# Sine passes of a gate side by side, and a second PSUM bank for the attention units of the lead

## The chip, the core and the metric

One core of a Trainium2 chip runs the kernel. The metric is the time of one execution on the device in microseconds, the median of several. Names of engines: PE is TensorE (PEld its weight loads), ACT ScalarE, DVE VectorE, POOL GpSimd, SP the queue that starts the transfers.

## What is computed

Three layers follow each other: attention that keeps the 32 best scores of each row, a layer with the activation h cos(h), and eight experts that all see every token, weighted by a matrix P that is normalised eight times by rows and columns.

```python
def _attn_ref(q, k, v):                      # (4, 8, 576, 64)
    scores = scale * np.matmul(q, k.transpose(0, 1, 3, 2))
    kth = np.partition(scores, -32, axis=-1)[..., -32:-31]
    scores = np.where(scores >= kth, scores, -1000000000.0)
    scores = scores - np.max(scores, axis=-1, keepdims=True)
    attn = np.exp(scores)
    attn = attn / (np.sum(attn, axis=-1, keepdims=True) + 1e-09)
    return np.matmul(attn, v)
...
x = attn_out.transpose(0, 2, 1, 3).reshape(2304, 512)
h = x @ w_in                                 # (512, 2048)
x = (h * np.cos(h)) @ w_out                  # (2048, 512)
...
for e in range(8):                           # w1 (8, 512, 1024), w2 (8, 1024, 512)
    out += P[:, e:e + 1] * (np.maximum(x @ w1[e], 0.0) @ w2[e])
```

## The kernel before

The 2304 tokens are 18 tiles of 128. The first three are the **lead** (LEAD = 3): their attention and their first layer run ahead of everything, in plain fp32, so that the experts have input early. The first layer's weights arrive in a wide format and are decoded meanwhile by DVE, ACT and POOL (lines 348 to 353) into win_s and wout_s.

An attention **unit** is one head of one tile: 128 rows of scores. A lead tile has eight units, and `att_tile` emits each: two score matmuls into the bank ps_s (line 469), each copied out by ACT (475); eight passes on DVE that find the 32nd largest score (477 to 481); two ACT passes that mask and exponentiate (483, 484); a normalisation on POOL (488); four transposes on PE into the bank ps_t and an ACT copy of them to at_f (493, 497); a fifth transpose of the last 64 columns into ps_t and its copy (the same lines); then, in `attention_tile`, five matmuls with the values, again into ps_t (550), and an ACT copy into the tile's x_f (554). Through ps_t each of these steps waits for the one before, and the next unit for this one.

The first layer of a lead tile is `moe1_tile_a` and `moe1_tile_b`. Part a multiplies x_f with win_s in four blocks of 512 columns, each four matmuls (647) and a copy to hs (649). Two blocks make one half of 1024 columns, and on each half runs `gate`: POOL, POOL and DVE reduce the angle (610 to 612), ACT takes the absolute value and the sine (613, 614), and DVE multiplies (617). Eight transposes of a half (657) and their copies (660) fill gT. Part b runs 16 matmuls with wout_s into the one bank y3 (669), copies the result (671), transposes it (676) and splits it into x2fh and x2fl (683, 684). Sine and exponential have different tables on ACT, so a sine between two exponentials brings two table loads.

When the three lead tiles are through, the **fill** (the experts on the lead's tokens, matmuls of lines 393 to 395) starts and gives PE work beside the attention of the other tokens; its first matmul reads x2fh of all three tiles. The attention of the other tokens uses buffers that are only free after the lead's last value product. Later, about 640 to 740 us, a part of the first layer for 512 tokens runs between two fills, with the attention beside it.

What sets the order is `Plan`: every instruction is put down with its engine, an assumed cost, the buffers (or parts of them) that it reads and writes, and a priority by engine and class of work (the table PRIORITY; smaller goes first). `issue` then walks through an assumed time, takes on each engine the ready instruction of the smallest priority, and writes the program out in the order so found. Where it sees PE without work in the first 230 us, it puts in **heartbeats**: single 128x128 matmuls of constants whose result nobody reads (`pl.beat`, line 1085), so many that they fill about 0.65 of the gap. At run time each engine follows its own list in order; the real waits are semaphores, which the framework below derives from the buffers.

Of the kernel before, what the change touches and what calls it, by code (L numbers as in the profile page):

```python
# [14 lines left out]
AF = mybir.ActivationFunctionType  # L15
# [12 lines left out]
CLASSES = ("first attention", "first mlp", "decode", "attention", "mlp")  # L28
PRIORITY = {
    "PE": (0, 1, 9, 0.5, 3),  # L30
    "ACT": (0, 0, 0, 2, 1.5),
    "DVE": (1, 0, 0.5, 2, 0),
    "POOL": (0, 0.5, 1, 1.5, 2),
    "SP": (0, 1, 0.5, 2, 3),
# [213 lines left out]
def fused_kernel(tc, kq, vv, w_in, w_out, w_gate, w1, w2, out, B=4):  # L248
# [32 lines left out]
    def put(eng, cost, emit, reads=(), writes=(), func=None, nbytes=0):  # L281
        return add(eng, cost, emit, reads, writes, PRIORITY[eng][CLASSES.index(work)], func, nbytes)
# [171 lines left out]
    def att_tile(stats, dests, plain=None):  # L454
# [34 lines left out]
        pt = lambda: ps_t.ap.rearrange("p (c t) -> p c t", c=4)  # L489
        for c0, c1, p in ((0, 4, 128), (4, 5, 64)):  # L490
            def tr(c0=c0, c1=c1, p=p):
                for c in range(c0, c1):
                    T_.transpose(pt()[:p, c - c0, :], ex.ap[:, c * 128 : c * 128 + p], ident.ap)  # L493

            put("PE", 109.0 * (c1 - c0), tr, [ex, ident], [ps_t])
            if plain:
                put("ACT", act_ns((c1 - c0) * 128, psum=True), lambda c0=c0, c1=c1, p=p: A_.activation(at_f.ap[:p, c0:c1, :], pt()[:p, 0 : c1 - c0, :], AF.Copy),
                    [ps_t], [(at_f, c0, c1)])
            for r0, rn, hd, t0 in dests:
                ath, atl = hd["ath"], hd["atl"]  # L500
                tv = slice(t0, t0 + rn)
                hv = lambda ath=ath, c0=c0, c1=c1, p=p, tv=tv: ath.ap[:p, c0:c1, tv]
                if c0:

                    lb, lv = ath, lambda ath=ath, tv=tv: ath.ap[64:128, 4:5, tv]
                else:
                    lb, lv = atl, lambda atl=atl, tv=tv: atl.ap[:, :, tv]
                sv = lambda c0=c0, c1=c1, p=p, r0=r0, rn=rn: pt()[:p, 0 : c1 - c0, r0 : r0 + rn]
# [20 lines left out]
    def attention_tile(t):  # L529

        nonlocal work
        work = "first attention"
        x_f, q = xf_r(), qp_r()
        s0 = t * 128
        dma(lambda: q.ap, lambda: kq[0:H, 0:64, 1, s0 : s0 + 128].rearrange("h d s -> d h s"), 1 << 18, writes=[q], slow=True)
        for pr in range(H // 2):
            k, v = kq_r(), vp_r()
            hs = slice(2 * pr, 2 * pr + 2)
            dma(lambda k=k, hs=hs: k.ap[0:64], lambda hs=hs: kq[hs, 0:64, 0, :].rearrange("h d s -> d h s"), 512 * S, writes=[k], slow=True)
            dma(lambda v=v: v.ap, lambda hs=hs: vv[hs].rearrange("h p c d -> p h c d"), 128 * 2560, writes=[v])  # L540
            for j in range(2):
                at_f = at_r()
                for _ in range(AHEAD[t]):
                    next(parts, None)
                att_tile([], [], dict(q=q, k=k, at=at_f, h=2 * pr + j))

                def av(v=v, j=j, at_f=at_f):
                    for c in range(5):
                        p = 64 if c == 4 else 128
                        T_.matmul(ps_t.ap[:64, :128], v.ap[:p, j, c, :], at_f.ap[:p, c, :], start=c == 0, stop=c == 4)  # L550

                put("PE", 1100.0, av, [v, at_f], [ps_t])
                r = slice(64 * j, 64 * j + 64)
                put("ACT", act_ns(128, psum=True), lambda pr=pr, r=r: A_.activation(x_f.ap[r, pr, :], ps_t.ap[:64, :128], AF.Copy), [ps_t], [(x_f, pr, pr + 1)])
        work = "mlp"
        return x_f

# [46 lines left out]
    def gate(hs, rr, n=1024):  # L604

        (hb, hv), (rb, rv) = hs, rr
        tt = tt_r()
        tv = lambda: tt.ap[:, :n]
        e, f, c = ("POOL", G_, 85.0 + 0.7 * n) if eng_r == "POOL" else ("DVE", V, dve_ns(n, True))
        put(e, c, lambda: f.tensor_scalar(tv(), hv(), 1.0 / TWO_PI, MAGIC, op0=ALU.mult, op1=ALU.add), [hb], [tt])  # L610
        put(e, c, lambda: f.tensor_scalar(rv(), tv(), -MAGIC, -TWO_PI, op0=ALU.add, op1=ALU.mult), [tt], [rb])
        put("DVE", dve_ns(n), lambda: V.tensor_tensor(rv(), rv(), hv(), op=ALU.add), [hb, rb], [rb])
        put("ACT", act_ns(n), lambda: A_.activation(rv(), rv(), AF.Abs), [rb], [rb])
        put("ACT", act_ns(n, ap=True), lambda: A_.activation(rv(), rv(), AF.Sin, scale=-1.0, bias=cols.ap[:, 0:1]), [rb, cols], [rb], func="sin")
        (hb, _, _), (rb, _, _) = hb, rb
# [20 lines left out]
    def moe1_tile_a(t, x_f):  # L636
# [1 line left out]
        nonlocal work  # L638
        work = "first mlp"
        gT = gT_r()  # L640
        for b0 in (0, 2):
            hs, rr = hs_r(), rr_r()
            for i in range(2):
                b = b0 + i
                pb = hb()
                for c in range(4):
                    put("PE", 4 * mm_ns(512), lambda c=c, b=b, pb=pb: T_.matmul(pb.ap, x_f.ap[:, c, :], win_s.ap[:, c, b * 512 : b * 512 + 512], start=c == 0, stop=c == 3),
                        [(win_s, c * 4 + b, c * 4 + b + 1), (x_f, c, c + 1)], [pb])
                put("ACT", act_ns(512, psum=True), lambda i=i, hs=hs, pb=pb: A_.activation(hs.ap[:, i * 512 : i * 512 + 512], pb.ap, AF.Copy), [pb], [(hs, i * 512, i * 512 + 512)])
            gate(wide_of(hs), wide_of(rr))  # L650
            for i in range(2):
                tb = trb()
                f = 4 * (b0 + i)
# [46 lines left out]
    def moe1(p, lag):  # L700
# [15 lines left out]
        for f0 in range(0, NF1, 2):  # L716
            hs, rr = hs_r(), rr_r()
            for i in range(2):
# [8 lines left out]
                if len(pend) > lag:  # L727
                    second(*pend.pop(0))
            gate(wide_of(hs, 2 * n), wide_of(rr, 2 * n), 2 * n)
            for i in range(2):  # L730
                gh, gl = gh_r(), gl_r()
                split_cols((gh, lambda gh=gh: gh.ap[:, :n]), (gl, lambda gl=gl: gl.ap[:, :n]), ((rr, i * n, i * n + n), lambda i=i, rr=rr: rr.ap[:, i * n : i * n + n]), n, eng=eng_g)
# [349 lines left out]
                for _ in range(4):  # L1082
                    next(sums, None)
    mixed_second(acc, *pend.pop(0))
    pl.beat = (lambda: T_.matmul(ps_g.ap[:, 0:128], ones.ap, ident.ap, start=True, stop=True)), 220.0, 230e3
    with tc.manual_schedule():
        pl.issue()
    pl.close()
# [35 lines left out]
```

## Time and profile before

| | |
|---|---|
| median of 3 runs | 2369.33 us (2368.64 to 2369.57) |
| profiled execution | 2372.1 us, of which span 2370.0 us |
| PE busy | 2326.2 us (98%) |
| DVE, ACT, POOL busy | 1817.3, 1357.3, 1243.0 us |
| mean granted PE clock | 0.995 |
| first fill matmul | 254.56 us after the span's start |

The rows further down come from one execution. Times are microseconds from the span's start unless marked ns. An engine's busy time in a stretch says how full it is; a bracket behind an instruction says how long its engine sat idle before it, and what ended that.

### The profile page before, as it was taken

How to read it: one execution, taken by the hardware profiler on the slowest of the kernel's cores; microseconds unless marked ns; L12 is line 12 of the kernel's file. 1: busy time of each engine (PE TensorE's matmuls, PEld its weight loads, DVE VectorE, ACT ScalarE, POOL GpSimd, SP SyncE). 2: the span in 40 equal slices, each digit the busy share in tenths (PEclk: the TensorE clock that was granted, in tenths of full speed). 3: DMA queues.
4: the chain of work that ended last, by engine and by line, in shares of the span. 5: the costliest groups of instructions: out<-in, count | busy, mean ns of one | idle time of the engine just before them, and what ended most of it. 6: DMA issues, size and time to landing. Idle time of an engine off the chain costs nothing.

```text
span 2370.0 us, 34117 instructions
## 1 busy us (share of the span) xinstructions
PE 2326.2 (98%) x11383; PEld 1923.5 (81%) x11383; DVE 1817.3 (77%) x3340; ACT 1357.3 (57%) x2724; POOL 1243.0 (52%) x1320
## 2 busy tenths in 40 slices
PE   7999999999989999999999999999999999999999
PEld 5555898988867888888888897888888888888887
DVE  6995999999989999994177786876666666666665
ACT  6987888888877777775376675222223222222221
POOL 6754878887886666664501036433333344444440
PEclk8999999999999999999999999999999999999999
DMA  8741555554432343333443432122222221111101
GB/s 254 218 137 36 167 157 158 158 168 153 141 93 83 119 120 120 118 93 107 125 125 103 121 117 70 41 76 76 77 84 78 79 67 36 36 36 36 36 23 49
DMA packets 152464, 242.27 MB, mean 102 GB/s; under 512 B 14624, under 2 KB 61808, under 8 KB 152288
## 3 DMA queue, kind: packets, MB, share of 16 engines
q1 hardware_dynamic: 152288, 240.10, 33.8%
q8 instruction: 89, 1.46, 0.3%
q14 instruction: 87, 0.71, 0.1%
HBM read 208.18 MB, written 31.87 MB: 101 GB/s over the span
## 4 chain that ended last, share of the span: by engine, by line
PE 84%; DVE 6%; POOL 4%; ACT 3%; DMA 2%; issue 1%; SPq 0%; POOLq 0%; DVEq 0%; ACTq 0%
PE y L393 12%; PE y L395 12%; PE y L394 12%; PE g L393 4%; PE g L395 4%; PE g L394 4%; PE t L493 3%; PE h L393 3%; PE h L395 3%; PE h L394 3%; PE t L519 1%; PE s L465 1%; PE y L404 1%; PE y L405 1%; PE y L408 1%
## 5 line engine op out<-in xcount | busy, mean ns | idle before, releaser
L368 POOL TENSOR_TENSOR wlo<-raw,whi 128x512 fp32r<-128x512 f32 x336 | 446.8, 1335 | 150.3 <-ACT whi L366 114.6
L481 DVE MAX8 m<-wk 128x8 f32<-128x576 f32 x432 | 319.3, 750 | 3.6
L968 DVE SCALAR_TENSOR_TENSOR acc<-y,P,acc 128x512 f32<-128x512 f32 x308 | 229.2, 748 | 103.6 <-PE y L395 103.4
L366 ACT ACTIVATE whi<-raw 128x512 fp32r<-128x512 f32 x416 | 258.1, 626 | 77.6 <-PE y L395 31.7
L480 DVE MATCH_REPLACE8 wk<-m,wk 128x576 f32<-128x576 f32 x288 | 214.2, 744 | 2.1
L393 PE MATMUL y<-whi,gh 128*128 128x512 f32 x448 | 181.8, 406 | 0.0
L395 PE MATMUL y<-whi,gl 128*128 128x512 f32 x448 | 176.2, 393 | 0.0
L393 PE MATMUL y<-gh,xh 128*128 128x512 f32 x450 | 175.9, 391 | 0.1
L394 PE MATMUL y<-wlo,gh 128*128 128x512 f32 x448 | 175.6, 392 | 0.0
L394 PE MATMUL y<-gl,xh 128*128 128x512 f32 x450 | 175.1, 389 | 0.0
L395 PE MATMUL y<-gh,xl 128*128 128x512 f32 x450 | 175.1, 389 | 0.0
L493 PE MATMUL t<-ident,ex 128*128 128x128 f32 (+1 forms) x720 | 128.0, 276 | 12.7 <-POOL ex L488 3.1
L475 ACT ACTIVATE sc<-s 128x288 f32<-128x288 f32 x288 | 116.1, 403 | 36.6 <-PE s L466 25.1
L488 POOL TENSOR_SCALAR ex<-ex,m 128x576 f32<-128x576 f32 x144 | 108.2, 751 | 45.4 <-DVE m L487 40.5
L493 PEld LDWEIGHTS t<-ident,ex 128*128 128x128 f32 (+1 forms) x720 | 84.5, 135 | 55.5 <-issue 9.4
L511 ACT ACTIVATE ath<-t 64x128 fp32r<-64x128 f32 (+3 forms) x272 | 104.5, 396 | 38.2 <-PE t L493 36.1
L477 DVE MAX8 m<-sc 128x8 f32<-128x576 f32 x144 | 107.5, 746 | 20.4 <-ACT sc L475 20.3
L483 ACT ACTIVATE ex<-sc,m 128x576 f32<-128x576 f32 x144 | 110.9, 770 | 18.4 <-DVE m L481 18.2
L484 ACT ACTIVATE ex<-ex,m 128x576 f32<-128x576 f32 x144 | 111.3, 773 | 4.6 <-POOL m L482 0.5
L480 DVE MATCH_REPLACE8 wk<-m,sc 128x576 f32<-128x576 f32 x144 | 106.9, 742 | 0.2
L393 PEld LDWEIGHTS y<-gh,xh 128*128 128x128 f32 x450 | 84.5, 188 | 18.6 <-DVE acc L964 0.8
L395 PE MATMUL y<-gh,gl 128*128 128x512 f32 x254 | 99.5, 392 | 0.0
(378 smaller groups left out, 7037.4 us busy)
## 6 DMA issues: line engine op xcount, KB each, us to landing
raw<-in_w_dram SPq DMA_DIRECT2D x384, 256.0 KB, 2.7
kq<-in_kq_dram SPq DMA_DIRECT2D x40, 576.0 KB, 3.9
raw<-win_d SPq DMA_DIRECT2D x64, 256.0 KB, 3.1
raw<-wout_d SPq DMA_DIRECT2D x64, 256.0 KB, 2.7
y_d<-st SPq DMA_DIRECT2D x56, 256.0 KB, 2.9
raw<-y_d SPq DMA_DIRECT2D x56, 256.0 KB, 2.7
d_raw<-in_w_in_dram SPq DMA_DIRECT2D x16, 512.0 KB, 5.2
d_raw<-in_w_out_dram SPq DMA_DIRECT2D x16, 512.0 KB, 4.4
```

What stands on the lines that cost most here:

```text
L366: put("ACT", act_ns(n), lambda: A_.activation(hv(), rv(), AF.Copy), [rb], [hb])
L368: put(e, c, lambda: f.tensor_tensor(lv(), rv(), hv().bitcast(F32), op=ALU.subtract), [rb, hb], [lb])
L393: T_.matmul(o(), ah(), bh(), start=start, stop=False)
L394: T_.matmul(o(), ah(), bl(), start=False, stop=False)
L395: T_.matmul(o(), al(), bh(), start=False, stop=stop)
L475: put("ACT", act_ns(288, psum=True), lambda c=c: A_.activation(sc.ap[:, c], o(), AF.Copy), [ps_s], [(sc, c.start, c.stop)])
L480: put("DVE", 669, lambda r=r, src=src: V.match_replace(wk.ap, mc(8 * r, 8), src.ap, LOWEST), [src, (m, 8 * r, 8 * r + 8)], [wk])
L481: put("DVE", 669, lambda r=r: V.max(mc(8 * r + 8, 8), wk.ap), [wk], [(m, 8 * r + 8, 8 * r + 16)])
L483: put("ACT", act_ns(S, ap=True), lambda: A_.activation(ex.ap, sc.ap, AF.Prelu, scale=-1.0, bias=mc(31), alpha=TINY), [sc, (m, 24, 32)], [ex])
L484: put("ACT", act_ns(S, ap=True) + 93.0, lambda: A_.activation(ex.ap, ex.ap, AF.Exp, scale=-0.125 / TINY, bias=mc(32), accum_out=mc(33)), [ ...
L493: T_.transpose(pt()[:p, c - c0, :], ex.ap[:, c * 128 : c * 128 + p], ident.ap)
L968: put("DVE", 663, lambda y=y, av=av, pcol=pcol: V.scalar_tensor_tensor(av(), y.ap, pcol(), av(), op0=ALU.mult, op1=ALU.add), [y, P, a], [a])
```

## The change

The gate is cut in two functions. `gate` now ends with the absolute value, and `gate_end` has the sine and the multiplication. A lead tile runs its four blocks and both `gate`s first, and then both `gate_end`s; the first sine is made to read the buffers of both halves (`also`), so that it waits for both absolute values. The priority of ACT's work of the class "first mlp" (the lead's first layer) goes from 0 to -1, ahead of the lead's attention. In the lead's units the fifth transpose goes to columns 0 to 255 of the bank ps_g, and the value product to columns 256 to 511 of it; ps_t keeps the first four transposes. Heartbeats, which wrote ps_g, now write columns 384 to 511 of ps_s, the bank of the scores. The later first layer calls both functions one behind the other.

```diff
-    "ACT": (0, 0, 0, 2, 1.5),
+    "ACT": (0, -1, 0, 2, 1.5),
...
         for c0, c1, p in ((0, 4, 128), (4, 5, 64)):
-            def tr(c0=c0, c1=c1, p=p):
+            bank = ps_g if plain and c0 else ps_t
+            pt = lambda bank=bank: bank.ap.rearrange("p (c t) -> p c t", c=4)
+
+            def tr(c0=c0, c1=c1, p=p, pt=pt):
...
-            put("PE", 109.0 * (c1 - c0), tr, [ex, ident], [ps_t])
+            put("PE", 109.0 * (c1 - c0), tr, [ex, ident], [(bank, 0, 256) if plain and c0 else bank])
...
-                        T_.matmul(ps_t.ap[:64, :128], v.ap[:p, j, c, :], at_f.ap[:p, c, :], start=c == 0, stop=c == 4)
+                        T_.matmul(ps_g.ap[:64, 256:384], v.ap[:p, j, c, :], at_f.ap[:p, c, :], start=c == 0, stop=c == 4)
...
         put("ACT", act_ns(n), lambda: A_.activation(rv(), rv(), AF.Abs), [rb], [rb])
-        put("ACT", act_ns(n, ap=True), lambda: A_.activation(rv(), rv(), AF.Sin, scale=-1.0, bias=cols.ap[:, 0:1]), [rb, cols], [rb], func="sin")
+
+    def gate_end(hs, rr, n=1024, also=()):
+
+        (hb, hv), (rb, rv) = hs, rr
+        put("ACT", act_ns(n, ap=True), lambda: A_.activation(rv(), rv(), AF.Sin, scale=-1.0, bias=cols.ap[:, 0:1]), [rb, cols, *also], [rb], func="sin")
...
-        for b0 in (0, 2):
-            hs, rr = hs_r(), rr_r()
...
-            gate(wide_of(hs), wide_of(rr))
+        halves = [(hs_r(), rr_r()) for _ in range(2)]
+        for b in range(4):
+            hs, rr = halves[b // 2]
...
+            if i:
+                gate(wide_of(hs), wide_of(rr))
+        for b0, (hs, rr) in zip((0, 2), halves):
+            gate_end(wide_of(hs), wide_of(rr), also=[wide_of(r)[0] for _, r in halves[1:]] if not b0 else ())
...
             gate(wide_of(hs, 2 * n), wide_of(rr, 2 * n), 2 * n)
+            gate_end(wide_of(hs, 2 * n), wide_of(rr, 2 * n), 2 * n)
...
-    pl.beat = (lambda: T_.matmul(ps_g.ap[:, 0:128], ones.ap, ident.ap, start=True, stop=True)), 220.0, 230e3
+    pl.beat = (lambda: T_.matmul(ps_s.ap[:, 384:512], ones.ap, ident.ap, start=True, stop=True)), 220.0, 230e3
```

The program's order changes with it on every engine. Three places follow. Line numbers move by some lines: 469, 475, 483 and 484 stay, 493 becomes 495, 497 becomes 499, 550 becomes 552, 554 becomes 556, 613 becomes 615, 614 becomes 620, 647 becomes 653, 649 becomes 655, 657 becomes 666, 660 becomes 669, 669 becomes 678, 1085 becomes 1095.

First, ACT around the gate of the second lead tile (tile 1), before. rr is the buffer of a gate half, ex and m belong to an attention unit, sc are scores, t and s are the banks:

```order
L613 ACTIVATE rr2_1239<-rr2_1239 128x1024
L475 ACTIVATE sc3_336<-s_119 128x288
L614 ACT_TABLE_LOAD
L614 ACTIVATE rr2_1239<-rr2_1239,cols_99 128x1024
L497 ACTIVATE at_f1_300<-t_255 128x512
L483 ACTIVATE ex0_191<-sc1_143,m1_82 128x576
L475 ACTIVATE sc3_336<-s_119 128x288
L497 ACTIVATE at_f1_300<-t_255 64x128
L484 ACT_TABLE_LOAD
L484 ACTIVATE ex0_191,m1_82<-ex0_191,m1_82 128x576
```

And after:

```order
L615 ACTIVATE rr0_717<-rr0_717 128x1024
L556 ACTIVATE x_f0_285<-g_261 64x128
L620 ACT_TABLE_LOAD
L620 ACTIVATE rr2_1178<-rr2_1178,cols_99 128x1024
L499 ACTIVATE at_f1_297<-t_254 128x512
L620 ACTIVATE rr0_717<-rr0_717,cols_99 128x1024
L499 ACTIVATE at_f1_297<-g_261 64x128
L483 ACTIVATE ex1_216<-sc2_282,m2_83 128x576
L484 ACT_TABLE_LOAD
L484 ACTIVATE ex1_216,m2_83<-ex1_216,m2_83 128x576
```

The first half's sine (rr2) has moved behind the second half's absolute value (rr0), the two sines have one copy between them, and one pair of loads serves both.

Second, PE at the same gate, before: from a unit's transposes to the value product two units later in the lead's last third. x_f0 and x_f are the inputs of the first layer, gT its gate's output, y1 and y2 banks for transposes of the gate:

```order
L657 MATMUL y1_900<-ident_90,rr2_1239 128x128 x4
L669 MATMUL y3_920<-wout_s_546,gT0_910 128x512
L493 MATMUL t_255<-ident_90,ex2_349 128x128 x4
L1085 MATMUL g_116<-ident_90,ones_88 128x128
L647 MATMUL h_339<-win_s_147,x_f0_289 128x512
L493 MATMUL t_255<-ident_90,ex2_349 64x128
L647 MATMUL h_339<-win_s_147,x_f0_289 128x512
L550 MATMUL t_255<-at_f0_262,vp0_106 64x128 x5
L669 MATMUL y3_920<-wout_s_546,gT1_1300 128x512 x2
L493 MATMUL t_255<-ident_90,ex0_191 128x128 x4
L669 MATMUL y3_920<-wout_s_546,gT1_1300 128x512 x3
```

And after, from the last in-projection matmul of tile 1 on:

```order
L678 MATMUL y3_884<-wout_s_548,gT0_874 128x512
L495 MATMUL t_254<-ident_90,ex2_357 128x128 x4
L495 MATMUL g_261<-ident_90,ex2_357 64x128
L653 MATMUL h_328<-win_s_146,x_f0_285 128x512 x2
L552 MATMUL g_261<-at_f0_263,vp0_106 64x128 x5
L1095 MATMUL s_116<-ident_90,ones_88 128x128 x3
L495 MATMUL t_254<-ident_90,ex0_190 128x128 x4
L495 MATMUL g_261<-ident_90,ex0_190 64x128
L1095 MATMUL s_116<-ident_90,ones_88 128x128 x10
L666 MATMUL y2_862<-ident_90,rr2_1178 128x128 x4
L552 MATMUL g_261<-at_f1_297,vp0_106 64x128 x5
```

The five transposes of a unit now stand together, and the transposes of the gate's first half (rr2) stand behind 13 heartbeats and in front of a value product; before, the first half's transposes stood ahead of these units, and five out-projection matmuls (669 with gT1) of that half among them.

Third, PE early in the lead, with the semaphore waits that the built program carries, before. kq and qp are keys and queries:

```order
L469 MATMUL s_119<-kq0_104,qp0_95 128x288 [waits DMAHW5_49,Activation_49]
L1085 MATMUL g_116<-ident_90,ones_88 128x128 x5
L469 MATMUL s_119<-kq0_104,qp0_95 128x288 [waits Activation_49]
L1085 MATMUL g_116<-ident_90,ones_88 128x128 x2
L493 MATMUL t_255<-ident_90,ex2_349 128x128 [waits Pool_49]
```

And after:

```order
L469 MATMUL s_116<-kq0_104,qp0_95 128x288 [waits DMAHW5_49]
L1095 MATMUL s_116<-ident_90,ones_88 128x128 [waits Activation_49]
L1095 MATMUL s_116<-ident_90,ones_88 128x128 x11
L469 MATMUL s_116<-kq0_104,qp0_95 128x288
L1095 MATMUL s_116<-ident_90,ones_88 128x128 [waits Activation_49]
L1095 MATMUL s_116<-ident_90,ones_88 128x128
L495 MATMUL t_254<-ident_90,ex2_357 128x128 [waits Pool_49]
```

The wait for ACT's copy of the scores has moved from the next score matmul to the heartbeats in front of it, which share its bank.

## Rows read from the trace of the kernel before

**Rows 1.** The page's head: the span, and each engine's busy time.

```profile
span 2370.0 us, 34117 instructions
PE 2326.2 (98%) x11383; PEld 1923.5 (81%) x11383; DVE 1817.3 (77%) x3340; ACT 1357.3 (57%) x2724; POOL 1243.0 (52%) x1320
```

**Rows 2.** Stretches: length, busy PE, PEld, DVE, ACT, POOL (count), clock, DMA, GB/s.

```profile
120.00:140.00 20.00, 20.00 (x92) 10.99 (x90) 19.38 (x43) 18.04 (x35) 9.20 (x15) 1.00 0.23 73
140.00:160.00 20.00, 20.00 (x79) 10.06 (x79) 18.40 (x36) 18.56 (x40) 15.03 (x18) 1.00 0.60 178
160.00:180.00 20.00, 20.00 (x81) 10.04 (x81) 17.62 (x37) 16.90 (x34) 9.35 (x14) 1.00 0.45 143
180.00:200.00 20.00, 19.86 (x97) 11.22 (x96) 7.55 (x14) 13.80 (x26) 5.57 (x8) 1.00 0.05 16
200.00:220.00 20.00, 17.95 (x51) 8.44 (x51) 8.55 (x15) 11.36 (x24) 10.43 (x13) 0.91 0.23 76
```

**Rows 3.** The same columns for two stretches of the body.

```profile
650.00:700.00 50.00, 44.24 (x196) 35.02 (x195) 43.35 (x58) 39.87 (x66) 42.87 (x33) 0.97 0.29 82
700.00:750.00 50.00, 44.59 (x222) 35.35 (x221) 43.18 (x82) 40.72 (x79) 32.76 (x36) 1.00 0.32 93
```

**Rows 4.** Groups of PE by line, 0 to 240 us: busy us, mean ns | idle.

```profile
L1085 PE MATMUL g<-ident,ones 128*128 128x128 f32 x210 | 37.2, 320 | 1.4 <-POOL ident masks.py:199 1.4
```

**Rows 5.** Groups of ACT by line, 0 to 240 us: the table loads.

```profile
L614 ACT ACT_TABLE_LOAD x6 | 7.7, 1283 | 0.1
L484 ACT ACT_TABLE_LOAD x6 | 7.7, 1283 | 0.2
```

**Rows 6.** Timelines of PE and ACT at the lead's last two units: start, us.

```profile
196.96 1.45 PE L550 MATMUL t<-at_f,vp 128*64 128x128 f32 x10
...
199.38 0.60 PE L493 MATMUL t<-ident,ex 128*128 128x128 f32 x4
...
200.68 0.29 PE L493 MATMUL t<-ident,ex 128*64 128x128 f32 x1
...
201.76 1.45 PE L550 MATMUL t<-at_f,vp 128*64 128x128 f32 x10
...
203.24 0.27 ACT L554 ACTIVATE x_f<-t 64x128 f32<-64x128 f32 x1 [1.97 <-PE t L550]
```

**Rows 7.** Timeline of DVE: the lead's last selection, and what comes next.

```profile
185.89 0.76 DVE L481 MAX8 m<-wk 128x8 f32<-128x576 f32 x1
...
203.30 0.61 DVE L1027 CAST qt<-zero 128x192 fp32r<-128x192 f32 x2 [7.62 <-PE t L550]
```

**Rows 8.** Timelines of PE and ACT at the second half of tile 1's gate.

```profile
176.32 1.02 PE L647 MATMUL h<-win_s,x_f 128*128 128x512 f32 x2
...
187.45 1.15 ACT L614 ACTIVATE rr<-rr,cols 128x1024 f32<-128x1024 f32 x1
188.50 0.58 ACT L497 ACTIVATE at_f<-t 128x512 f32<-128x512 f32 x1
...
189.43 1.20 PE L657 MATMUL y<-ident,rr 128*128 128x128 f32 x8
```

**Rows 9.** Timeline of PE from the last value product to the first fill matmul.

```profile
212.84 0.40 PE L465 MATMUL s<-kh,qs 128*128 128x288 f32 x1 [2.04 <-POOL qs L449]
...
229.67 2.74 PE L669 MATMUL y<-wout_s,gT 128*128 128x512 f32 x6
...
240.06 1.88 PE L669 MATMUL y<-wout_s,gT 128*128 128x512 f32 x4
...
253.67 0.23 PE L625 MATMUL y<-x2fl,wg 128*8 128x128 f32 x1 [1.36 <-DVE x2fl L684]
...
254.56 0.39 PE L393 MATMUL g<-x2fh,whi 128*128 128x384 f32 x1
```

**Rows 10.** Waits of PE, 0 to 120 us: in total, times, longest.

```profile
PE s L469 <- ACT sc L475: 4.2, 7, 1.4
...
PE t L493 <- ACT at_f L497: 1.8, 2, 1.0
PE t L493 <- ACT x_f L554: 1.5, 1, 1.5
```

More of the change, by code (lines that the diff above doesn't have):

```diff
@@ L488, in att_tile @@
         put("POOL", 724, lambda: G_.tensor_scalar(ex.ap, ex.ap, mc(35), 0.0, op0=ALU.mult, op1=ALU.add), [ex, (m, 35, 36)], [ex])
-        pt = lambda: ps_t.ap.rearrange("p (c t) -> p c t", c=4)
         for c0, c1, p in ((0, 4, 128), (4, 5, 64)):
-            def tr(c0=c0, c1=c1, p=p):
+            bank = ps_g if plain and c0 else ps_t
+            pt = lambda bank=bank: bank.ap.rearrange("p (c t) -> p c t", c=4)
+            def tr(c0=c0, c1=c1, p=p, pt=pt):
                 for c in range(c0, c1):
                     T_.transpose(pt()[:p, c - c0, :], ex.ap[:, c * 128 : c * 128 + p], ident.ap)
-            put("PE", 109.0 * (c1 - c0), tr, [ex, ident], [ps_t])
+            put("PE", 109.0 * (c1 - c0), tr, [ex, ident], [(bank, 0, 256) if plain and c0 else bank])
             if plain:
-                put("ACT", act_ns((c1 - c0) * 128, psum=True), lambda c0=c0, c1=c1, p=p: A_.activation(at_f.ap[:p, c0:c1, :], pt()[:p, 0 : c1 - c0, :], AF.Copy),
-                    [ps_t], [(at_f, c0, c1)])
+                put("ACT", act_ns((c1 - c0) * 128, psum=True), lambda c0=c0, c1=c1, p=p, pt=pt: A_.activation(at_f.ap[:p, c0:c1, :], pt()[:p, 0 : c1 - c0, :], AF.Copy),
+                    [(bank, 0, 256) if c0 else bank], [(at_f, c0, c1)])
             for r0, rn, hd, t0 in dests:
@@ L507, in att_tile @@
                     lb, lv = atl, lambda atl=atl, tv=tv: atl.ap[:, :, tv]
-                sv = lambda c0=c0, c1=c1, p=p, r0=r0, rn=rn: pt()[:p, 0 : c1 - c0, r0 : r0 + rn]
+                sv = lambda c0=c0, c1=c1, p=p, r0=r0, rn=rn, pt=pt: pt()[:p, 0 : c1 - c0, r0 : r0 + rn]
                 k = (c1 - c0) * rn
@@ L549, in av @@
                         p = 64 if c == 4 else 128
-                        T_.matmul(ps_t.ap[:64, :128], v.ap[:p, j, c, :], at_f.ap[:p, c, :], start=c == 0, stop=c == 4)
-                put("PE", 1100.0, av, [v, at_f], [ps_t])
+                        T_.matmul(ps_g.ap[:64, 256:384], v.ap[:p, j, c, :], at_f.ap[:p, c, :], start=c == 0, stop=c == 4)
+                put("PE", 1100.0, av, [v, at_f], [(ps_g, 256, 512)])
                 r = slice(64 * j, 64 * j + 64)
-                put("ACT", act_ns(128, psum=True), lambda pr=pr, r=r: A_.activation(x_f.ap[r, pr, :], ps_t.ap[:64, :128], AF.Copy), [ps_t], [(x_f, pr, pr + 1)])
+                put("ACT", act_ns(128, psum=True), lambda pr=pr, r=r: A_.activation(x_f.ap[r, pr, :], ps_g.ap[:64, 256:384], AF.Copy), [(ps_g, 256, 512)], [(x_f, pr, pr + 1)])
         work = "mlp"
@@ L640, in moe1_tile_a @@
         gT = gT_r()
-        for b0 in (0, 2):
-            hs, rr = hs_r(), rr_r()
[L643 to L649, printed above, removed]
-            gate(wide_of(hs), wide_of(rr))
+        halves = [(hs_r(), rr_r()) for _ in range(2)]
+        for b in range(4):
+            hs, rr = halves[b // 2]
+            i = b % 2
+            pb = hb()
+            for c in range(4):
+                put("PE", 4 * mm_ns(512), lambda c=c, b=b, pb=pb: T_.matmul(pb.ap, x_f.ap[:, c, :], win_s.ap[:, c, b * 512 : b * 512 + 512], start=c == 0, stop=c == 3),
+                    [(win_s, c * 4 + b, c * 4 + b + 1), (x_f, c, c + 1)], [pb])
+            put("ACT", act_ns(512, psum=True), lambda i=i, hs=hs, pb=pb: A_.activation(hs.ap[:, i * 512 : i * 512 + 512], pb.ap, AF.Copy), [pb], [(hs, i * 512, i * 512 + 512)])
+            if i:
+                gate(wide_of(hs), wide_of(rr))
+        for b0, (hs, rr) in zip((0, 2), halves):
+            gate_end(wide_of(hs), wide_of(rr), also=[wide_of(r)[0] for _, r in halves[1:]] if not b0 else ())
             for i in range(2):
```

## The prediction

> **What bounds the kernel now.** I read the page's engine shares first, then the table of 20 us stretches, then the timelines of PE, DVE and ACT around the end of the lead. TensorE is busy 98% of the span [rows 1], so the kernel can only gain where TensorE works on nothing of use: it idles, or it runs heartbeats. Two places hold most of that. The lead (the first 255 us) has 210 records of heartbeats before 240 us, two to a matmul, 37.2 us in all or 0.35 us a heartbeat [rows 4], beside plain idle time. The stretch from 650 to 750 us has 11.2 us of idle time (44.24 and 44.59 of 50) [rows 3]. From 120 to 200 us TensorE is full, with hardly a heartbeat, while DVE is nearly full until 180 [rows 2]: there the lead is bound by TensorE, and a wait added there is paid in full. After 180 us DVE empties (7.55 and 8.55 of 20) [rows 2]: its last selection step of the lead ends at 186.65, and the next attention's work, which may only start when the lead's last value product is done, begins at 203.30 [rows 7]. The body starts with the first fill matmul at 254.56 [rows 9].
>
> **The table loads.** The two halves of a tile's gate each load the sine table and the exponential table again: 6 and 6 loads of 1.283 us in the lead [rows 5]. The order has 3 and 3 afterwards, so ACT loses 7.7 us of work. This is not on TensorE's path by itself: ACT has gaps in the same stretches (18.04 of 20 between 120 and 140, 13.80 between 180 and 200) [rows 2]. I take nothing for it directly; what it can buy is that copies which TensorE waits for come sooner, and that is inside the first term below.
>
> **The second bank.** Before, a unit's four transposes, its fifth, and its value product all use ps_t, each after an ACT copy. Where units follow without other work between, this chain sets their distance: value products at 196.96 and 201.76, 4.80 apart, and the last unit's first transpose comes at 199.38, when the bank is free [rows 6]. Afterwards the first four use ps_t alone. What stays serial is the fifth transpose (200.68), its copy, the product (201.76) and the copy of that (203.24, 0.27 long): 2.8 us by the same rows [rows 6]. So up to 2.0 us a unit can go, where nothing else holds it. Ahead of 120 us, TensorE's named waits on this chain are 1.8 us (for at_f) and 1.5 us (for x_f) [rows 10]; they go. The order also has nine heartbeats fewer ahead of the twelfth value product (91 against 100), at most 0.35 us each: 3.2 us, half of which I count, since DVE rather than TensorE sets the pace there. **Against it** stands that the heartbeats now write ps_s, the bank of the scores: in the order, 21 of their 36 groups carry a wait on ACT, and none did before. Behind such a group stand transposes and value products that did not wait for the scores' copy. What TensorE waited for that copy so far is 4.2 us [rows 10]; I price the new waits between 0 and 4.2 and take 2, as most of these groups stand where the next score matmul waited for the same copy. Term one: -3.3 - 1.6 + 2 = **-3 us**, bounds -6 and +1.
>
> **The sine pair in tile 1.** Now the first sine waits for the Abs of the second half, so no half of the gate is through before both. In the order, the transposes of tile 1's first gate half stand behind 1 out-projection matmul, 2 in-projection matmuls, 10 transposes, 1 value product and 13 heartbeats, counted from the tile's last in-projection matmul. From that matmul to the transposes of the half that it completes, the trace shows 177.34 (its end) to 189.43: 12.1 us, through copy, GpSimd, DVE, Abs, load, sine and product [rows 8]. A projection matmul costs 0.86 us (2.74 for three less 1.88 for two) [rows 9]; a value product is 1.45, and a unit's transposes are 0.60 and 0.29 [rows 6]. The useful work in front is 3 x 0.86 + 1.45 + 2 x 0.89 = 5.8 us. The rest, 12.1 - 5.8 = **+6.3 us**, is heartbeats and idling in a stretch that held 0.14 us of idle time [rows 2]. Behind the waiting transposes, in TensorE's own queue, stand the value products of the lead's last three units, and those are what DVE waits for at 203.30 [rows 7]. The second sine comes one sine and one copy later (187.45 to 188.50, 1.05, and 0.58) [rows 8]. Bounds: 0, if the earlier work lets the matmul in question come sooner by as much, and +8.
>
> **What is moved behind.** Ahead of the last lead unit's value product the order has 35 and 19 projection matmuls (in, out) where it had 37 and 25: 8 fewer, 6.9 us of work [rows 9] that now lies in the tail, between that product and the first fill matmul. There TensorE used to wait 2.04 us for GpSimd and 1.36 us for DVE [rows 9], ran six heartbeats behind the last tile, and in the 20 us with the first of these waits the mean granted clock was 0.91, so part of them ran at 1.2 instead of 2.4 GHz [rows 2]. More ready work covers more of that: **-3 us**, bounds 0 and -6. Tile 2's own pair costs nothing there: its out-projection had to wait for tile 1's bank in any case, and 13 matmuls of tile 1 stand in front of its transposes.
>
> **The body.** The order has the same 7296 split matmuls of the body, in another order. After the transposes of unit 31 it has 54 of them done where it had 75; attention runs ahead of the fill by 21 matmuls, at most 0.39 us each [rows 9]. When the stretch that used to idle (650 to 750 us) comes, TensorE then has some fill left. I take -2.5 of its 11.2 us [rows 3], bounds 0 and -6; a schedule made anew can also lose there, which the range takes in.
>
> **The sum.** -3 + 6.3 - 3 - 2.5 = -2.2 us. The profiled execution took 2372.1 us (span 2370.0 and 2.1 around it), 2.8 above the median 2369.33; against the median the forecast is **2367 us**. The measurement can tell about 0.2% from no change, 4.7 us, so this is "same".
>
> **The rivals.**
> A, faster. The matmul work of tile 1 is early enough that the gate's 12.1 us are covered (its +6.3 becomes 0), and attention gets ahead so far that the body's idle stretch gives 4 us. For it: the chain of 4.80 us a unit [rows 6], and the 16.6 us from DVE's last selection to 203.30 [rows 7]. Against it: TensorE is full before that gate, so its matmuls can't come much sooner. -3 + 0 - 3 - 4 = -10: 2359 us. The Trainium skill, Perfetto Trace Analysis, section Optimizing Tensor Performance, speaks for it: independent matmul groups should rotate through banks so that the reading of one overlaps the next. By that rule alone the sum would be nearer to -10.
> B, slower. The pair's wait in tile 1 stands at its full +6.3, and the other three terms come to nothing: the early part is set by DVE and the loading of weights, the tail keeps its waits, and the body's idle stretch its length. It decides if tile 1's first gate transposes start 12 us or more behind its last in-projection matmul: 2376 us.
> C, the change does not do what it says. The fifth transpose of the next unit and the value product of this one share ps_g in different columns, and the order has waits on ACT at the fifth transposes. The copy of the product ends 0.3 us behind it (203.21 to 203.51) [rows 6], and the next unit's four transposes cover about as much; with ACT's queue in between I take 0.4 us for each of the 12 last units, 5 us, on top of the forecast's sum: 2372 us. The Trainium skill, PSUM - Partial Sum Buffer, section Terms, says that TensorE and ScalarE may not use one bank in the same 32 partitions at once. By that rule the two halves of ps_g are no two banks, and the heartbeats can't run while the scores are copied; no row of before shows either, since ps_g and ps_s were not shared so.
>
> **How the numbers follow.** Forecast 0.45, A 0.27, B 0.18, C 0.10. From 2357 (A with somewhat more in the body) to 2378 (B with bounds of +8 and +1): some 0.08 are left out on either side. Faster by over 0.2% (under 2364.6): A and a little of the forecast, 0.29. Slower (over 2374.1): B, part of C and a little of the forecast, 0.25. Same: 0.46.
>
> **What would show it.** Right: six sine and exponential loads fewer on ACT before 240 us; the last value product of the lead 0 to 4 us sooner than 201.76; a hole of some 4 us or its heartbeats on TensorE in front of tile 1's gate transposes; the first fill matmul within 254 to 260 us; less than 11 us idle between 640 and 750. Wrong: a first fill matmul before 250 us (A), or after 262 (B, C); heartbeats that wait for ACT by more than 4 us in total; a body whose idle time changes by more than 6 us either way, since of its new order I have only counts.

## The result, and the profile of the changed kernel

The changed kernel takes 2385.98 us (median of 4, 2381.64 to 2387.84), the kernel before beside it 2369.45: a ratio of 1.0061, interval 1.0041 to 1.008. It is 16.5 us slower, outside the range of the prediction. In what follows (+x) behind a time is its distance from the median of the kernel before, run beside it on the same chip.

The page's head of the changed kernel answers [rows 1]; under it the groups of PE and ACT by line from 0 to 255 us, which answer [rows 4, 5]:

```profile
span 2385.7 us, 34084 instructions
PE 2331.9 (98%) x11389; PEld 1929.5 (81%) x11389; DVE 1821.1 (76%) x3340; ACT 1350.8 (57%) x2718; POOL 1241.2 (52%) x1320
...
L1095 PE MATMUL s<-ident,ones 128*128 128x128 f32 x216 | 41.0, 340 | 15.6 <-ACT sc L475 14.2 <-POOL ident masks.py:199 1.4
L620 ACT ACT_TABLE_LOAD x3 | 3.8, 1283 | 0.1
L484 ACT ACT_TABLE_LOAD x3 | 3.8, 1283 | 0.1
```

The loads went from six and six to three and three. The heartbeats, which had waited 1.4 us in all, now wait 15.6, of which 14.2 for ScalarE's copy of the scores. Two stretches of 50 us in the body, one fill matmul, and the end of the lead on DVE and PE answer [rows 3, 6, 7, 9]:

```profile
650.00:700.00 50.00, 42.73 (x195) 33.91 (x194) 46.98 (x67) 39.27 (x65) 40.42 (x35) 0.97 0.24 72
700.00:750.00 50.00, 45.02 (x213) 35.65 (x213) 38.95 (x58) 43.50 (x76) 39.09 (x36) 1.00 0.32 93
...
213.38 1.45 PE L552 MATMUL g<-at_f,vp 128*64 128x128 f32 x10
...
272.12 0.40 PE L393 MATMUL g<-x2fh,whi 128*128 128x384 f32 x1
...
214.91 0.61 DVE L1037 CAST qt<-zero 128x192 fp32r<-128x192 f32 x2 [4.63 <-PE g L552]
```

The lead's last value product starts at 213.38 instead of 201.76, the first fill matmul at 272.12 instead of 254.56. The body idles as before (12.25 of these 100 us against 11.2). So in this execution the whole loss is made in the lead (the fill starts 17.6 us later, the span is 15.7 us longer), and two thirds of it ahead of 213 us. The waits of PE from 0 to 120 us answer [rows 10], and below them stand the stretches from 40 to 60 us of before and of after (length, PE, PEld, DVE, ACT, POOL, clock, DMA, GB/s):

```profile
PE s L1095 <- ACT sc L475: 13.1, 15, 3.5
...
PE s L469 <- ACT sc L475: 0.9, 1, 0.9
```

```profile
40.00:60.00 20.00, 17.85 (x92) 12.33 (x90) 15.86 (x34) 18.20 (x36) 17.48 (x18) 0.92 0.89 277
```

```profile
40.00:60.00 20.00, 15.49 (x52) 9.59 (x51) 11.85 (x23) 11.50 (x22) 10.80 (x12) 0.64 0.63 210
```

The score matmuls' own waits for that copy fell from 4.2 to 0.9 us, the heartbeats' rose from none to 13.1. Every engine is emptier at 40 to 60 us, DVE by 4 us, and the granted clock is 0.64, so TensorE ran a good part of the stretch at 1.2 instead of 2.4 GHz.

### The profile page after: what moved, and what is told of

It is laid out like the page before. It is cut to its first block, busy times and chain, and to the rows that moved or that the text cites. A ratio compares the mean times of both kernels' runs of the same rounds, so it can differ in the third digit from the quotient of the medians.

```text
span 2385.7 us, 34084 instructions
## 1 busy us (share of the span) xinstructions
PE 2331.9 (98%) x11389; PEld 1929.5 (81%) x11389; DVE 1821.1 (76%) x3340; ACT 1350.8 (57%) x2718; POOL 1241.2 (52%) x1320
## 4 chain that ended last, share of the span: by engine, by line
PE 82%; DVE 9%; ACT 4%; POOL 3%; issue 1%; DMA 1%; SPq 0%; POOLq 0%; ACTq 0%; DVEq 0%
PE y L393 11%; PE y L395 11%; PE y L394 11%; PE g L395 3%; PE g L393 3%; PE g L394 3%; PE t L495 3%; PE h L395 2%; PE h L394 2%; PE h L393 2%; DVE wk L480 2%; PE y L408 2%; DVE m L481 2%; PE y L405 2%; PE y L404 2%
## 5 line engine op out<-in xcount | busy, mean ns | idle before, releaser
L495 PE MATMUL t<-ident,ex 128*128 128x128 f32 (+1 forms) x696 | 121.5, 276 | 16.4 <-DVE ath L514 6.7
```

## The experiments

Three parts can be told apart: the bank that the heartbeats write, ScalarE's priority with the sine pair, and the units' second bank.

**1. The heartbeats' bank alone.** One line in the kernel before; the order on every engine is the same, instruction for instruction.

```diff
-    pl.beat = (lambda: T_.matmul(ps_g.ap[:, 0:128], ...
+    pl.beat = (lambda: T_.matmul(ps_s.ap[:, 384:512], ...
```

> The kernel before with one change: its heartbeats write columns 384 to 511 of ps_s instead of ps_g; every instruction stands in the same order. Theory H (the heartbeats' bank: heartbeats that wait for the scores' copies cost the early lead): slower than before by 8 to 15 us, 2377 to 2384, waits of heartbeats on ACT of some 10 us ahead of 120 us, and the twelfth value product at 128 us or later instead of 122.5. Theory S (the sine pair) and theory B (fifth transpose and value product sharing a bank): no more than 2 us slower, 2371 at most.

Measured: 2378.42 us (+8.3; ratio 1.0026, 1.0007 to 1.0045). The heartbeats wait 13.8 us for the scores' copies by 120 us; the eighth value product comes at 95.0 us, and the first fill matmul at 261.1, each some 6.5 us late. TensorE idles 23.4 us up to 120 us, where it idled 18.0, at the same mean clock of 0.94: the loss is idle time. ScalarE's waits for PE up to 120 us show how it spreads, before and then in this run:

```profile
ACT sc L475 <- PE s L469: 9.2, 4, 5.8
...
ACT at_f L497 <- PE t L493: 1.6, 3, 0.8
```

```profile
ACT sc L475 <- PE s L469: 14.2, 7, 6.0
ACT at_f L497 <- PE t L493: 7.8, 9, 2.8
```

The score matmuls and transposes stand behind heartbeats that wait, and ScalarE then waits for both: 11.2 us more in all.

**2. The sine pair with the priority, and the second bank with the heartbeats in the scores' bank.** The first takes the gate and ScalarE's priority from the change and leaves the units and heartbeats as before; the second the reverse.

> The changed kernel without its second bank: the units use ps_t alone, the heartbeats ps_g, as before; the two sines stand together. H and B: within 4 us of the kernel before, 2366 to 2374. S: slower by 8 us or more, 2378 or more. My recorded sum priced the pair's wait in tile 1 at +6.3 us, less what the tail gives back: 2372.

> The changed kernel with the gate as before (each half through to its sine, ACT's priority as before); units on two banks, heartbeats on ps_s. H: slower by 8 to 15 us, 2377 to 2384, with over 8 us of heartbeats waiting for ACT. S: within 4 us of the kernel before. B: slower, with the idle time at transposes and value products rather than at heartbeats.

Measured: gate and priority 2376.91 us (+6.8; 1.0014 to 1.0034), second bank with heartbeats 2379.33 (+9.2; 1.0025 to 1.0046). The sum of the two is +16.0, beside the +16.5 of the change. The first lies between what theory S and its rivals forecast. It loses nothing ahead of the lead's last value product, which starts at 200.8 us, 1.0 sooner than before; its first fill matmul comes at 257.6, 3.0 later.

**3. The whole change with the heartbeats on a bank of their own.** All eight banks are in use, so one is freed: the gate's transposes use one bank instead of two by turns.

```diff
-    hb, trb = Cycle([ps_y[0], ps_h]), Cycle([ps_y[2], ps_y[1]])
+    hb, trb = Cycle([ps_y[0], ps_h]), Cycle([ps_y[2]])
...
-    pl.beat = (lambda: T_.matmul(ps_s.ap[:, 384:512], ...
+    pl.beat = (lambda: T_.matmul(ps_y[1].ap[:, 0:128], ...
```

> The changed kernel with its heartbeats in a bank that no unit uses: all transposes of the gates go through y2, and the heartbeats write y1. H: 10 to 15 us faster than the changed kernel, 2369 to 2375; no heartbeat waits. S and B: within 3 us of the changed kernel, 2381 to 2388. One bank instead of two for the gates' transposes should cost up to 2 us.

Measured: 2374.28 us (+4.2; 1.0003 to 1.0026), first fill matmul at 256.3. The heartbeats' bank is worth 12 of the 16.5 us, and more if the single bank for the gate's transposes costs something (part 4). PE's timeline around 50 us shows how; first the changed kernel (start, us; in the bracket the idle time ahead and what ended it), then this run:

```profile
48.84 0.75 PE L469 MATMUL s<-kq,qp 64*128 64x288 f32 x2
53.10 5.16 PE L1095 MATMUL s<-ident,ones 128*128 128x128 f32 x24 [3.51 <-ACT sc L475]
58.19 0.75 PE L469 MATMUL s<-kq,qp 64*128 64x288 f32 x2
```

```profile
44.64 0.75 PE L469 MATMUL s<-kq,qp 64*128 64x288 f32 x2
45.32 2.94 PE L1095 MATMUL y<-ident,ones 128*128 128x128 f32 x24
49.48 0.75 PE L469 MATMUL s<-kq,qp 64*128 64x288 f32 x2 [1.21 <-ACT sc L475]
```

It is the same gap between two score matmuls. With a bank of their own the heartbeats run while ScalarE copies, and the gap is 4.84 us. In the scores' bank they wait for the copy, run after it, and only then comes the score matmul that waited for nothing but that copy: 9.35 us. The 24 records take 5.16 us after 3.5 us of idling and 2.94 without, so the wait has also cost clock, which heartbeats are there to keep: the granted clock was 0.55 from 53.1 to 58.3 us in the changed kernel, and 1.00 from 45.3 to 48.3 in this run.

**4. Without the gate's part, and without heartbeats.** The second bank with a free heartbeat bank, gate and priority as before; then the change and the kernel before with no heartbeats (they compute nothing); then the kernel before with one bank for the gate's transposes, as a control.

```diff
-    pl.beat = (...), 220.0, 230e3
+    pl.beat = (...), 220.0, 0.0
```

> The units' fifth transpose and value product use the second bank, as in the change; the gate is as before (each sine pass where it stood, ScalarE's priority for the first MLP back at 0); the leading gates' transposes all use one bank (y2), and the heartbeats the bank that this frees (y1). Against the run with the whole change and the same free bank (2374.28 us) it lacks the sine pair alone; against the run with the second bank and the heartbeats in the scores' bank (2379.33 us) it lacks the heartbeats' waits alone. Theory H (nearly all the harm is the heartbeats' bank, and the sine pair's share is what the run with the sine pair alone showed, about +6.5 us): 2368 to 2371 us, no heartbeat waits for ScalarE beyond the masks' one, first fill matmul at 252 to 256 us. Theory B (sharing the second bank between transpose and value product costs something itself): 2373 us or more, with waits of the fifth transpose for the product's copy to x_f. Theory S' (the sine pair costs nothing once heartbeats are free, and the remaining +4 us is the one bank of the gate's transposes): 2374 us as with the sine pair.

> The whole change, with no heartbeats at all (the 58 matmuls that only keep TensorE at work are left out; the output is the same). Theory Q (the heartbeats in the scores' bank cost because score matmuls queue behind them): the heartbeat waits (13.1 us by 120 us) are gone, value product 8 comes at 88 to 92 us instead of 97.65, and the time is 2372 to 2380 us. Theory C (what costs is the clock that falls while TensorE idles, 0.64 of full between 40 and 60 us): without heartbeats the clock is lower still (under 0.6 from 20 to 100 us) and the time is no better than with them, 2386 us or more.

> The kernel before with no heartbeats at all. It gives what heartbeats on a bank of nobody else's are worth, which bounds what they can lose by being late. Theory Q: they are worth little, 2368 to 2376 us, since VectorE sets the pace of the early lead and does the same work. Theory C: without them the clock stays near half until the gates fill TensorE, and the time rises to 2378 us or more; then a late heartbeat costs by the clock as well as by the queue.

> The kernel before, with the leading gates' transposes all on one bank (y2) instead of two by turns; the heartbeats stay on the bank they had. A control for the runs that free the other bank. If the one bank costs nothing: 2369 to 2371 us, first fill matmul at 254 to 256 us. If it does (a gate transpose waits for ScalarE to have copied the one before): 2373 to 2375 us with 2 to 4 us of waits of the gate's transposes for gT, and then the run with the whole change and a free bank owes its +4 us to this and not to the sine pair.

Measured: second bank with free heartbeats 2367.27 us (-3.2; 0.9964 to 0.9993), quicker than both kernels. Without heartbeats the change takes 2383.39 (+12.9), the kernel before 2377.08 (+6.6). So heartbeats are worth 6.6 us in the kernel before and lose all of it in the scores' bank (+8.3). In the change they are worth 9 us on a bank of their own (2374.28) and nothing in the scores' bank (2385.98). Both times lie between the ranges of the two theories, so neither queueing nor the clock alone accounts for them; these runs do not say how large each share is. The control, 2375.11 (0.9999 to 1.0035), is unclear: the single bank may cost some us, which the second bank's gain would then have paid.

**5. Is it the scores' bank, or any bank that is read?** The heartbeats go to columns 384 to 511 of ps_g, the units' second bank, in the whole change and with the second bank alone. Both orders are unchanged against the scores' bank.

> The whole change, with the heartbeats in columns 384 to 511 of the units' second bank g, which the fifth transpose (0 to 255) and the value product (256 to 383) leave free, instead of columns 384 to 511 of the scores' bank. Nothing else is changed. Theory H (a heartbeat waits whenever ScalarE still has to read its bank, so its cost goes with how long that bank's copies are awaited): the waits for the scores' copies (13.1 us by 120 us) go, and waits for the copies out of g (line 499 and line 556) come in their place, 2 to 6 us in all; first fill matmul at 256 to 262 us; time 2372 to 2378 us, of which +7 us over the kernel before is the sine pair. If instead any shared bank costs alike, it stays at 2383 us or more.

> The second bank alone (gate and ScalarE's priority as before, the gates' transposes on two banks by turns), with the heartbeats in columns 384 to 511 of the units' second bank g. Theory H: like the run with the second bank and a free heartbeat bank (2367.27 us), within the heartbeats' new waits for the copies out of g: 2365 to 2372 us. If the sine pair's price is the same with it as without (+7 us), this run is 6 to 8 us below the whole change with the same heartbeat bank. If any shared bank costs alike, it is at 2377 us or more, as with the scores' bank (2379.33 us).

Measured: 2388.17 us (+18.8) and 2377.78 (+8.4), no better than the scores' bank, though the waits up to 120 us are fewer (6.0 and 5.7 us). My expectation that the price follows the sum of the waits fell; where a wait stands matters more. The whole change, PE and then ACT around tile 1's gate:

```profile
195.37 0.27 PE L495 MATMUL g<-ident,ex 128*64 128x128 f32 x1
199.11 4.63 PE L1095 MATMUL g<-ident,ones 128*128 128x128 f32 x20 [3.46 <-ACT at_f L499]
203.53 1.06 PE L666 MATMUL y<-ident,rr 128*128 128x128 f32 x4
...
196.23 1.15 ACT L620 ACTIVATE rr<-rr,cols 128x1024 f32<-128x1024 f32 x1
197.28 0.58 ACT L499 ACTIVATE at_f<-t 128x512 f32<-128x512 f32 x1
197.76 1.14 ACT L620 ACTIVATE rr<-rr,cols 128x1024 f32<-128x1024 f32 x1
198.80 0.26 ACT L499 ACTIVATE at_f<-g 64x128 f32<-64x128 f32 x1
```

The heartbeats wait until ScalarE, after both sines, copies the fifth transpose out of their bank; then 20 records run at half pace, and the gate's transposes stand behind them, although DVE's product that they need started at 198.25.

**6. Where is the sine pair's price?** On the free heartbeat bank, the pair in tiles 0 and 1 only, and in tile 2 only.

```diff
-            gate_end(..., also=[...] if not b0 else ())
+            gate_end(..., also=[...] if not b0 and t < 2 else ())     # the other: t == 2
```

> The whole change with the heartbeats on the bank that the gate's transposes give up (as in the run of 2374.28 us), but in tile 2 the first sine no longer waits for the second half's Abs, so its two sines stand apart again; tiles 0 and 1 keep the pair. Against that run it takes away tile 2's pair alone, against the run without any pair (2367.27 us) it adds tiles 0 and 1's. Theory T (the pair's price of about 7 us is paid in the tail: in the run with the sine pair alone tile 2's last gate transposes came at 231.78 instead of 228.69 and the first fill matmul 3.0 us later, while the lead's last value product was 1.0 us sooner): 2367 to 2371 us, first fill matmul at 253 us. Theory S (as in the prediction: the pair costs in tile 1, where TensorE is full, and nothing in tile 2): 2373 to 2376 us, first fill matmul at 256 to 258 us.

> The counterpart: the same kernel with the pair in tile 2 alone; the sines of tiles 0 and 1 stand apart. Theory T: nearly the whole price, 2371 to 2375 us, first fill matmul some 3 us later than in the counterpart. Theory S: none, 2366 to 2370 us, and the last value product of the lead 1 to 6 us sooner than with the pairs of tiles 0 and 1. If both come out between, the price is shared, or lies in ScalarE's raised priority for the first MLP, which both keep and the run without any pair does not have.

Measured: 2378.54 us (+7.5) and 2375.48 (+4.5): each costs no less than the pair in all three tiles (+4.2), and the first even 3 us more, which no theory here foresaw. The price does not go with the place, so something that both kept was suspected: ScalarE's priority.

**7. Priority and pair apart.** On the free heartbeat bank, priority without pair, pair without priority, neither; and the priority alone in the kernel before.

```diff
-    "ACT": (0, 0, 0, 2, 1.5),
+    "ACT": (0, -1, 0, 2, 1.5),
```

> The second bank with the heartbeats on the free bank and no sine pair (2367.27 us), and ScalarE's priority of the first MLP at -1 as in the change. Theory P (the priority is what costs: ScalarE takes the gate's copies and Abs ahead of the scores' and units' copies, which the selection and so VectorE wait for): 2372 to 2376 us. Theory S (the pair costs, wherever it stands): 2366 to 2369 us. Theory O (every new order of the lead shifts the time by some us, this one had a good draw): anything from 2367 to 2376 us, without a pattern between the four runs.

> The whole change with the heartbeats on the free bank (2374.28 us), but ScalarE's priority of the first MLP back at 0: the pair alone. Theory P: 2366 to 2369 us. Theory S: 2372 to 2376 us.

> The second bank with a free heartbeat bank, no pair, priority 0, once more on this chip, as the point from which the other two are counted and as a second look at whether it beats the kernel before: 2365 to 2369 us, 2 to 4 us under the kernel before.

> The kernel before with the one number of ScalarE's priority changed, 0 to -1. Theory P: 2374 to 2378 us, as in the run with gate and priority together (2376.91 us). Theory S: 2368 to 2372 us.

Measured, with the second bank in all of the table:

| heartbeats | | priority 0 | priority -1 |
|---|---|---|---|
| free bank | no pair | 2366.38 (-3.6) | 2371.64 (+1.7) |
| free bank | pair | 2368.39 (-1.6) | 2374.28 (+4.2) |
| scores' bank | no pair | 2379.33 (+9.2) | not run |
| scores' bank | pair | 2378.33 (+7.8) | 2385.98 (+16.5) |

The priority costs 5.3 and 5.8 us on the free bank. The pair's 2.0 and 2.5 are not clear of the scatter (0.9985 to 1.0004 with the pair and priority 0, 0.9969 to 0.9998 with neither). The priority alone costs +3.1 in the kernel before (1.0001 to 1.0022), between the two theories; of the 6.8 us of gate and priority together (part 2) that leaves 3.7 for the pair there. The second bank with neither is 3.6 us quicker than the kernel before a second time (0.9969 to 0.9998). DVE with the priority (no pair), and then the stretch from 100 to 120 us without it and with it:

```profile
106.31 0.76 DVE L481 MAX8 m<-wk 128x8 f32<-128x576 f32 x1
...
111.21 0.16 DVE L487 RECIPROCAL m<-m 128x1 f32<-128x1 f32 x1 [1.40 <-POOL m L486]
114.63 1.29 DVE L623 TENSOR_TENSOR rr<-rr,hs 128x512 f32<-128x512 f32 x2 [3.26 <-ACT rr L620]
116.00 0.76 DVE L477 MAX8 m<-sc 128x8 f32<-128x576 f32 x1
```

```profile
100.00:120.00 20.00, 19.04 (x87) 10.92 (x87) 18.68 (x39) 18.48 (x36) 14.60 (x18) 1.00 0.64 194
```

```profile
100.00:120.00 20.00, 17.45 (x83) 9.91 (x81) 13.75 (x26) 18.07 (x34) 9.01 (x12) 1.00 0.11 27
```

From 92 to 113 us ScalarE copies scores eight times without the priority and twice with it (93.00 and 111.75), since tile 0's gate goes first. DVE does no selection from 107.1 to 116.0 and is busy 13.75 instead of 18.68 us. Tile 0's first gate transposes come at 103.4 instead of 122.1, the lead's last value product at 205.9 instead of 196.8.

That gap is not yet the price. The first fill matmul of the run without the priority, of the run with it, and of part 4's run, which is the kernel without it in another execution:

```profile
250.83 0.39 PE L393 MATMUL g<-x2fh,whi 128*128 128x384 f32 x1
...
251.07 0.39 PE L393 MATMUL g<-x2fh,whi 128*128 128x384 f32 x1
...
255.63 0.39 PE L393 MATMUL g<-x2fh,whi 128*128 128x384 f32 x1
```

The tail gives back what the gap took, and the spans of the first two, 2361.9 and 2369.2 us, part only behind the fill's start. From 255 to 1800 us TensorE idles 18.0 us in both; from 640 to 800 the granted clock is 1.00 and 0.98. With the pair the fill starts level too (256.62 without the priority, 256.32 with it). So on the free bank the medians show that the priority costs, and no run shows by which path. Nor is theory O, that each new order shifts the time by some us, put aside: the priority costs in every pair of runs, but part 6 has 3 us that neither the pair nor the priority explains.

**8. Do the parts add, and what of the opposite priority?** The whole change with priority 0, heartbeats in the scores' bank; and the second bank with a free heartbeat bank, no pair, and priority 0.5.

> The whole change, heartbeats in the scores' bank as in it, with ScalarE's priority of the first MLP back at 0. If the parts add (priority 5 to 6 us whatever the heartbeats' bank): 2379 to 2382 us, with waits of heartbeats for the scores' copies as in the change (11 to 15 us by 120 us). If the heartbeats' waits hide it: 2384 us or more.

> The second bank with a free heartbeat bank and no pair (2366.38 us with priority 0, 2371.64 us with -1), with ScalarE's priority of the first MLP at 0.5, behind the lead's attention. Theory P as a direction (copies of scores that come late starve the selection): 2362 to 2367 us, no gap of VectorE's selection like the one of 7 us between 108 and 116 us with -1. If 0 is already the best place (the gate then comes too late for the tail): 2368 us or more.

Measured: 2378.33 us (+7.8; the heartbeats wait 14.4 us by 120 us), so the priority costs 8.7 us there and does not hide behind the heartbeats; here the fill does start later with it, at 272.12 instead of 263.75. Priority 0.5 gives 2380.37 (+9.8; 1.0027 to 1.0057), and my direction was too simple. PE of that run, its first gate transposes, its last value product and its first fill matmul:

```profile
154.64 0.66 PE L664 MATMUL y<-ident,rr 128*128 128x128 f32 x4
...
181.40 1.45 PE L552 MATMUL g<-at_f,vp 128*64 128x128 f32 x10
...
273.15 0.63 PE L393 MATMUL g<-x2fh,whi 128*128 128x384 f32 x1
```

The attention is through 15 us sooner (196.84 with priority 0), but tile 0's gate comes 32 us later, and the gates then stand in the tail: 91.8 us from the last product to the fill, 54.0 with priority 0. Of the three values tried, zero is the quickest.

## Why the prediction was wrong

**The step that failed most is the heartbeats in term one.** I priced their new waits between 0 and 4.2 us and took 2, since most would replace a wait of the next score matmul for the same copy. That is what happened to the wait: 4.2 us became 0.9 there. But the heartbeats' own run time, which lay beside the copy, now lies behind it and in front of that matmul, and every engine gets its work later. It measured 8.3 us alone, and 9.4 to 12.8 us with the second bank (7.8 against -1.6, 9.2 against -3.6, 16.5 against 4.2). The prediction's sentence that DVE sets the pace of the early lead was no reason to count little, since DVE's own work hangs on those copies. By 120 us DVE had waited 12.8 us for them in the kernel before, 14.4 with the heartbeats' bank alone and 19.6 in the changed kernel; the last figure takes the priority as well, for with priority 0 and the heartbeats in the scores' bank (part 8) it is 12.4. The idle time of TensorE, 18.0 against 23.4 us, tells the loss better.

**ScalarE's priority had no term.** It stood in the diff, and I took it as part of the gate's new place. It cost 3.1 to 8.7 us in the four places where it was tried apart, in three of them more than the pair that it came with; by which path stays open.

**The sine pair** I put at +6.3 in tile 1. The hole itself came: in front of tile 1's first gate transposes (201.82) stand 3.3 us of heartbeats and 1.6 us of idling. But the pair cost 2.0 and 2.5 us where it can be told apart from the priority on the free bank, within the scatter, and 3.7 in the kernel before; +7.8 against +9.2 in the scores' bank shows no price. The loads saved are worth nothing visible.

**The second bank** I put at -3.3 of waits and -1.6 of heartbeats. With the heartbeats out of the way it gives -3.2 and -3.6. The 3.3 us of waits on the chain became 0.3 and 1.3, and TensorE's idle time up to 120 us 13.9 and 13.5 instead of 18.0: the mechanism holds, and the size as far as one bank for the gate's transposes costs nothing. The Trainium skill, Perfetto Trace Analysis, section Optimizing Tensor Performance, asks for groups that rotate through banks; the runs agree with it, at 3 to 4 us.

**The tail** was to give -3. From the last value product to the first fill matmul it took 52.8 us before and 58.7 after: no gain. **The body** was to give -2.5 and idles 12.25 instead of 11.2 us: also none. Both rested on counts of instructions in the order, and no row showed that the counted work would fill an idle place.

**The rivals.** B's sum (2376) took the pair for the cause and was short by ten; its sign, 12 us or more from tile 1's last in-projection matmul to its gate's first transposes, did not come either (9.9 us, 191.89 to 201.82). C had the right place in half a sentence, that heartbeats can't run while the scores are copied, but its price went to ps_g. The Trainium skill, PSUM — Partial Sum Buffer, section Terms, says that two engines may not use one bank in the same 32 partitions at once. The traces agree in effect: columns 384 to 511 waited for readers of columns 0 to 287. The waits are the program's semaphores, so no run here shows what the bank itself would have done. The signs that were to show the forecast wrong did show it: heartbeats waiting more than 4 us (14.2), a fill after 262 (272.12).

The parts on the free bank add up: -3.6 + 5.3 + 2.0 = 3.7, measured 4.2. The heartbeats' 12.3 us are what is left to 16.5, so that step tests nothing. What stays open: by which path the priority costs; what one bank for the gate's transposes costs; and why the pair in two tiles (+7.5) or one (+4.5) costs no less than in all three (+4.2). Every change of the order shifts later work as well; 640 to 800 us held 16.7, 9.9 and 13.8 us of idle time in these three.

## What to carry to other kernels

Filler work must own what it touches: put behind a buffer that another engine still reads, it is not free, since it waits first and then makes the useful work behind it wait for its run time too. Price such a move as the filler's run time laid end to end with the wait, not as the wait alone. And give every number in a diff its own term and its own run: here a single priority, which had no term, cost as much as the rearrangement that it came with or more, and the quickest version measured was the change without both. A gap that one trace shows is not yet a price either: look whether a later landmark, such as the first fill matmul, still carries it.

## What was not expected of the hardware

Behind 3.51 us of idling, 24 heartbeat records took 5.16 us at a granted clock of 0.55; behind a busy stretch they took 2.94 us at 1.00. Executions of one kernel differ by the clock as well: of 31 executions of the kernel before, one had a mean granted clock of 0.996 and a span of 2364.8 us, another 0.986 and 2381.7. The second bank with the free heartbeat bank ran twice under the profiler with the same order on every engine: from 80 to 100 us the granted clock was 0.66 once and 1.00 once, and the first fill matmul came at 255.63 and 250.83 us. A landmark in a single trace can so be off by some 5 us, and sums of a few us are better made on medians.
